# Chunked attention and two MLPs on one core: the order of the first pieces, and the engine of one conversion step

## The chip, the cores and the metric

The kernel runs on one core of a Trainium2 chip. The metric is the device time of one execution in microseconds (us); the median of several runs is given. The core's engines are TensorE (PE), VectorE (DVE), ScalarE (ACT), GpSimd (POOL) and SyncE (SP). Each runs its own instructions in the order in which the program issued them and waits at semaphores for the others; SP and POOL here mostly issue DMA transfers.

## What is computed

```python
# q, k, v: (4, 8, 576, 64); attention within chunks of 64 rows
scores = scale * q_c @ k_c.T ; attn = softmax(scores) ; out = attn @ v_c
x = out.transpose(0, 2, 1, 3).reshape(2304, 512)
# first MLP, d_ff = 1536
x = ((x @ w_a) * (x @ w_b)) @ w_out
# second MLP, d_ff = 2048, g a rational function of h
h = x @ w_in
g = (a0 + a1*h + a2*h*h + a3*h*h*h) / (1 + |b0|*|h| + |b1|*h*h + 1e-6)
return g @ w_out2
```

Weights come in 64 bits (f64 on the host) and are turned into f32 on the core.

## The kernel before

**Arithmetic.** A product of the MLPs is made of three passes: each operand is split into a high part (a rounded copy, ScalarE) and a low part (what is left, VectorE), and `mm3` (lines 250 to 252) adds high x high, high x low and low x high.

**Attention** goes in 18 units of 128 tokens (two chunks, eight heads). A unit's steps, with their letters in the table FIRST: k and q are transposed on TensorE and copied by ScalarE (line 328 and 330, letters k and q, copies kT and qT), scores are multiplied (345) and VectorE takes the row maximum and subtracts it (351, 353; S), ScalarE takes the exponential (359; X), VectorE sums and divides (364 to 367; E), the probabilities are transposed (375) and copied to pT (377; P), multiplied with v (392; V), with the high part of x copied by ScalarE (408), and the low part follows on VectorE (412; L). Units 0 to 2 are done ahead of the main loop; units 3 to 5 lie between its products.

**Weights.** A tile of weights is loaded as raw 64-bit words into one of four buffers (AHEAD = 4; SP queue, line 170) and converted in four pieces by `w_piece` (line 199; letter w): piece 0 makes two terms of the raw words, z on ScalarE (215) and c, the exponent term, on ScalarE (217) or VectorE (219); piece 1 takes the high part of the tile before (192, ScalarE) and shifts c (222, VectorE); piece 2 makes the last bits (224, ScalarE), takes the low part of the tile before (197, VectorE) and asks for another load; piece 3 adds the terms to an f32 tile (232, VectorE), which POOL stores to DRAM (234). A load into a raw buffer waits until the tile that lay there has been through pieces 0 and 2. Tiles are numbered in their order of use: tile 0 is the first of w_a, 1 the first of w_b, 2 the second of w_a, and so on; the number stands in the name of a converted tile (`w_a_2_361` is tile 2).

**Order.** The schedule is by hand: what the Python code issues first stands first in an engine's queue. Ahead of the main loop it is the table LOADS (first loads on SP) and then the table FIRST (lines 80 to 83). In FIRST a letter with a number is a step of a unit, `w` is the next piece of weights, `d4` is four idle products of the identity with itself on TensorE (`warm`, line 803), and `+k5` is a load. The main loop (885) makes, for each of the first pairs of tiles, the half products `ab` of w_a (a_s, the copy of it by ScalarE, line 888) and of w_b, 12 passes each; in the middle of each and after each stands `half()` (875), a stop at which the next pieces of weights and the due steps of attention are issued. How many pieces have been issued by stop n is in line 880.

**After 60 us** come the rest of attention, the second part of the first MLP and the second MLP, which the change does not touch.

Of the kernel before, what the change touches and what calls it, by code (L numbers as in the profile page):

```python
# [20 lines left out]
def chunk_attention_two_mlps(  # L21
# [56 lines left out]


    FIRST = (  # L80
        "k0 d2 q0 w w S0 w X0 k1 d2 w E0 q1 w S1 X1 P0 w k2 q2 E1 V0 w S2 X2 L0 P1 w +k5 +q5 w V1 d4 E2 w w +v3 +v4 +v5 "
        "L1 d2 P2 d4 w w V2 d4 L2 w w"
    ).split()
    LOADS = "k0 q0 w k1 q1 v0 w k2 q2 v1 w v2 w k3 q3 k4 q4".split()

    AHEAD = 4
    NWP = 12 - AHEAD
    AN = 1280

    SIZES = [256, 512, 512, 512, 512]  # L90
    START = [sum(SIZES[:j]) for j in range(len(SIZES))]
# [50 lines left out]
    order1 = [(n, i) for i in range(F1) for n in ("a", "b")]  # L142
    ordero = [("o", i) for i in range(F1)]
# [29 lines left out]
    def w_tile(key, dtype):  # L173
        at = w_at[key]
        if at < len(order1):
            pool, tag = p_w, f"w{at % NWP}"
        elif at < len(order1) + len(ordero):
            pool, tag = p_w, f"w{at - len(order1)}"
        else:
            pool, tag = p_w2, f"v{at - len(order1) - len(ordero)}"  # L180
        t = pool.tile([P, 2, DM], dtype, name=f"w_{key[0]}_{key[1]}_{at}", tag=tag)
        return t[:, 0], t[:, 1]

    def w_fetch_ahead(n):
        while n_cv[0] < n_cv[2] and n_cv[0] < n + (AHEAD if n_cv[0] < len(order1) else 2):
            w_fetch()

    def w_hi(n):
        if n in f32s:
            key = order[n]  # L190
            wt[key] = w_tile(key, F32R)
            nc.scalar.copy(wt[key][0], f32s[n].bitcast(F32))

    def w_lo(n):
        if n in f32s:
            hi, lo = wt[order[n]]
            nc.vector.tensor_tensor(lo, f32s.pop(n).bitcast(F32), hi.bitcast(F32), ALU.subtract)

    def w_piece():


        n, piece = divmod(n_cv[1], 4)
        n_cv[1] += 1
        key = order[n]
        if piece == 0:
            w_fetch_ahead(n)
            t = raws.pop(key)

            terms[n] = (t, *w_tile(key, I32))
        t, c, z = terms[n]  # L210
        hw = t[:, :, 1]
        lw = t.rearrange("p f t -> p (f t)").bitcast(U16).rearrange("p (f t) -> p f t", t=4)[:, :, 1]
        zz = z.bitcast(F16).rearrange("p (f t) -> p f t", t=2)
        if piece == 0:
            nc.scalar.activation(zz[:, :, 1], hw.bitcast(F32), AF.Copy, scale=2.0 ** -112)
            if 0 < n < len(order1) + len(ordero):
                nc.scalar.activation(c.bitcast(F32), hw.bitcast(F32), AF.Copy, scale=2.0 ** -112)
            else:
                nc.vector.tensor_scalar(c.bitcast(F32), hw.bitcast(F32), 2.0 ** -112, None, ALU.mult)
        elif piece == 1:  # L220
            w_hi(n - 1)
            nc.vector.tensor_scalar(c, c, 3, None, ALU.logical_shift_left)
        elif piece == 2:
            nc.scalar.activation(zz[:, :, 0].bitcast(U16), lw, AF.Copy, scale=2.0 ** -13)
            w_lo(n - 1)
            if n < len(order1):
                w_fetch_ahead(n + 1)
        else:
            w_fetch_ahead(n + 1)
            del terms[n]  # L230
            x = f32s[n] = p_io.tile([P, DM], I32, name="w_x", tag="io")
            nc.vector.tensor_tensor(x, c, z, ALU.add)
            if key in w1_d:
                nc.gpsimd.dma_start(out=w1_d[key], in_=x.bitcast(F32))

    def w_until(tiles):

        while n_cv[1] < min(4 * tiles, 4 * n_cv[2]):
            w_piece()

    def w_flush():

        n = n_cv[1] // 4 - 1
        if n in f32s:
            w_hi(n)
            w_lo(n)
# [20 lines left out]
    def tick(dt):  # L267

        now[0] += dt
        while todo:  # L270
            nxt = min(todo, key=lambda t: t[:2])
            if nxt[0] > now[0] + 1e-6:
                break
            todo.remove(nxt)
            nxt[2]()
# [363 lines left out]
    def a_tile(n):  # L639
        at = n_a[0] if n_a[0] + n <= AN else 0  # L640
        n_a[0] = at + n
        return a_ring[:, at:at + n]
# [232 lines left out]
    def half():  # L875


        n = n_half[0]
        n_half[0] += 1
        w_until(min(15 + 2 * n, 32) / 4 if n < 17 else (n + 18) / 4)  # L880
        if n_cv[1] == 32 or n_cv[1] == 4 * len(order1):
            w_flush()
        tick(0.5)
# [79 lines left out]
    for n, (j, i) in enumerate(places):  # L963
# [17 lines left out]
        if j == NB - 1:  # L981
# [4 lines left out]
            if i >= F1 - EARLY:  # L986
                if a_ring is None:
                    w_flush()
                    s_cv.close()
                    p_a = ctx.enter_context(tc.tile_pool(name="a", bufs=1, side="right", reuse_waits="tile"))  # L990
                    a_ring = p_a.tile([P, AN], F32, name="a_ring", tag="a_ring")
                step2(i - (F1 - EARLY))
# [32 lines left out]
```

## Time and profile before

| | us |
|---|---|
| median of 3 runs | 917.63 (916.88 to 918.42) |
| profiled execution | 916.23 |
| its span, first to last instruction | 914.5 |
| TensorE busy | 890.3 (97%) |
| VectorE busy | 722.2 (79%) |
| ScalarE busy | 612.9 (67%) |

The profile is one execution. The span is from the first to the last instruction, and the profiled execution's own time is 1.7 us longer. TensorE is busy nearly all the time; where it waits, and for whom, is read from the views by time, of which the rows are shown below.

### The profile page before, as it was taken

To read this page: it belongs to the slowest core of one execution; us is meant where nothing else is said; L and a number is where in the kernel's file an instruction comes from. 1 tells how busy PE (TensorE), PEld (TensorE's weight loads), DVE (VectorE), ACT (ScalarE), POOL (GpSimd) and SP (SyncE) were. 2 spreads that over 40 slices of the span, in tenths; PEclk is the share of its full clock that TensorE was granted. 3 is DMA by queue.
4 is the path that set the end of the run, shared out by engine and by line. 5 is a ranking of instruction groups with operands and counts; after the bars stand their busy time and mean duration, and the time that the engine had idled before them with its cause. 6 is when DMAs were issued, how large, how long until landed. Compare 5 with 4: busy or idle time off the path is not lost.

```text
span 914.5 us, 14768 instructions
## 1 busy us (share of the span) xinstructions
PE 890.3 (97%) x5532; PEld 787.9 (86%) x5532; DVE 722.2 (79%) x1321; ACT 612.9 (67%) x1105; POOL 63.8 (7%) x122
## 2 busy tenths in 40 slices
PE   5989999999999999999999999999999999999998
PEld 4888989989999999888886899888888888888997
DVE  6657788488888785677766599999889988988886
ACT  6757888355554552667766588877677767677775
POOL 0111111111111111000000000000000000000000
PEclk9999999999999999999999999999999999999999
DMA  9959996234343413777767110110020002000100
GB/s 244 272 174 256 255 237 169 95 127 153 122 144 121 149 57 111 257 246 252 256 228 252 60 46 1 40 42 1 1 92 1 1 1 80 1 1 1 47 1 35
DMA packets 107336, 105.82 MB, mean 116 GB/s; under 512 B 61441, under 2 KB 84481, under 8 KB 107265
## 3 DMA queue, kind: packets, MB, share of 16 engines
q1 hardware_dynamic: 99264, 79.71, 29.8%
q0 software_dynamic: 8000, 25.17, 7.7%
q8 instruction: 43, 0.70, 0.3%
q14 instruction: 29, 0.23, 0.1%
HBM read 74.98 MB, written 29.88 MB: 115 GB/s over the span
## 4 chain that ended last, share of the span: by engine, by line
PE 90%; DVE 3%; DMA 3%; ACT 2%; issue 1%; SPq 0%; DVEq 0%; ACTq 0%
PE acc L251 7%; PE h L252 7%; PE h L250 7%; PE h L251 7%; PE acc L250 7%; PE acc L252 7%; PE acc L668 5%; PE acc L669 5%; PE acc L674 5%; PE ab L250 4%; PE ab L251 3%; PE ab L252 3%; PE y L251 2%; PE y L250 2%; PE y L252 2%; PE q L250 2%
## 5 line engine op out<-in xcount | busy, mean ns | idle before, releaser
L252 PE MATMUL h<-y,w_i 128*128 128x512 f32 (+1 forms) x320 | 118.0, 369 | 0.0
L250 PE MATMUL h<-y,w_i 128*128 128x512 f32 (+1 forms) x320 | 117.9, 368 | 0.0
L251 PE MATMUL h<-y,w_i 128*128 128x512 f32 (+1 forms) x320 | 117.8, 368 | 0.0
L732 ACT ACTIVATE a_ring<-h 128x512 f32<-128x512 f32 (+1 forms) x80 | 44.1, 552 | 88.6 <-PE h L252 88.6
L668 PE MATMUL acc<-g_hi,w_o 128*128 128x512 f32 (+1 forms) x240 | 88.9, 377 | 2.8 <-ACT g_hi L654 2.1
L576 ACT COPY s<-y 128x384 f32<-128x384 f32 x72 | 34.5, 479 | 80.2 <-PE y L252 79.0
L669 PE MATMUL acc<-g_hi,w_o 128*128 128x512 f32 (+1 forms) x240 | 87.4, 371 | 0.0
L735 DVE SCALAR_TENSOR_TENSOR u<-u,cb_t,a_ring 128x512 f32<-128x512 f32 (+1 forms) x80 | 55.7, 696 | 30.8 <-ACT u L733 29.9
L251 PE MATMUL acc<-w_o,g_hi 128*128 128x512 f32 x191 | 75.3, 394 | 0.0
L250 PE MATMUL acc<-w_o,g_hi 128*128 128x512 f32 x191 | 74.9, 392 | 0.0
L252 PE MATMUL acc<-w_o,g_lo 128*128 128x512 f32 x191 | 74.3, 389 | 0.0
L250 PEld LDWEIGHTS h<-y,w_i 128*128 128x128 f32 x320 | 60.1, 188 | 8.9
L251 PEld LDWEIGHTS h<-y,w_i 128*128 128x128 f32 x320 | 60.1, 188 | 8.7
L252 PEld LDWEIGHTS h<-y,w_i 128*128 128x128 f32 x320 | 60.1, 188 | 7.4
L656 DVE TENSOR_TENSOR g_lo<-g_raw,g_hi 128x512 fp32r<-128x512 f32 (+1 forms) x60 | 38.0, 636 | 31.8 <-ACT g_hi L654 17.7
L674 PE MATMUL acc<-g_lo,w_o 128*128 128x512 f32 (+1 forms) x237 | 59.9, 374 | 0.7 <-DVE g_lo L656 0.6
L734 ACT ACTIVATE t<-h,ca_t 128x512 f32<-128x512 f32 (+1 forms) x80 | 59.0, 738 | 0.0
L745 DVE SCALAR_TENSOR_TENSOR u<-u,r 128x512 f32<-128x512 f32 (+1 forms) x80 | 50.5, 632 | 9.5 <-ACT r L744 9.5
L737 DVE SCALAR_TENSOR_TENSOR t<-t,ca_t,h 128x512 f32<-128x512 f32 (+1 forms) x80 | 55.5, 694 | 2.8
L668 PEld LDWEIGHTS acc<-g_hi,w_o 128*128 128x128 f32 x240 | 45.1, 188 | 13.9 <-ACT g_hi L654 4.5
L744 ACT ACTIVATE r<-r,nlsh 128x512 f32<-128x512 f32 (+1 forms) x80 | 54.6, 682 | 2.6
L743 ACT ACTIVATE r<-u,nlsh 128x512 f32<-128x512 f32 (+1 forms) x80 | 55.5, 694 | 0.3
(195 smaller groups left out, 2415.5 us busy)
## 6 DMA issues: line engine op xcount, KB each, us to landing
w_raw<-in_moe_w_out_dram SPq DMA_DIRECT2D x28, 512.0 KB, 3.7
g_d<-g POOLq DMA_DIRECT2D x72, 192.0 KB, 2.5
g_raw<-g_d SPq DMA_DIRECT2D x48, 256.0 KB, 4.0
w_raw<-in_moe_w_in_dram SPq DMA_DIRECT2D x16, 512.0 KB, 3.9
w_raw<-in_moe_w_a_dram SPq DMA_DIRECT2D x12, 512.0 KB, 5.1
w_raw<-in_moe_w_b_dram SPq DMA_DIRECT2D x12, 512.0 KB, 5.1
out_dram<-o SPq DMA_DIRECT2D x18, 256.0 KB, 2.4
y_d<-ys POOLq DMA_DIRECT2D x16, 256.0 KB, 3.7
```

The lines of the kernel that those rows point to most:

```text
L250: nc.tensor.matmul(ps, wh, xh, start=first, stop=False, **kw)
L251: nc.tensor.matmul(ps, wh, xl, start=False, stop=False, **kw)
L252: nc.tensor.matmul(ps, wl, xh, start=False, stop=last, **kw)
L668: nc.tensor.matmul(acc[j][d], wh, gh, start=i == 0, stop=False)
L669: nc.tensor.matmul(acc[j][d], wl, gh, start=False, stop=False)
L674: nc.tensor.matmul(acc[j][d], cols(w, d)[0], gl, start=False, stop=last)
L734: nc.scalar.activation(t, ps, AF.Identity, scale=ca_t[:, 3:4], bias=ca_t[:, 2:3])
L735: nc.vector.scalar_tensor_tensor(u, u, cb_t[:, 0:1], ah, ALU.add, ALU.mult)
L737: nc.vector.scalar_tensor_tensor(t, t, ca_t[:, 1:2], ps, ALU.add, ALU.mult)
L743: nc.scalar.activation(r, u, AF.Ln, scale=2.0 ** -LSH, bias=nlsh[:, 0:1])
L744: nc.scalar.activation(r, r, AF.Exp, scale=-1.0, bias=nlsh[:, 1:2])
L745: nc.vector.scalar_tensor_tensor(u, u, 1.0 + 1e-6, r, ALU.add, ALU.mult)
```

## The change

Three things are altered.

1. The table FIRST, from P1 on: the two pieces of weights that stood ahead of V1 and its idle products now stand behind the normalisation of unit 2 (E2), so E2 comes two pieces earlier, and P2 and V2 come earlier against the pieces too; the loads of v for units 3 to 5 now come ahead of the pieces that ask for tiles 6 and 7. The idle products behind V1, P2 and V2 become 2, 1 and 2; they were 4 and 2, 4, and 4. The count of pieces, 15, is the same.
2. Line 880: by each stop of the main loop up to the 32nd piece, two more pieces have been issued.
3. The exponent term c of tiles 2 to 5 is made by VectorE instead of ScalarE (`C_ACT` lists the tiles that stay on ScalarE).

```diff
     FIRST = (
-        "k0 d2 q0 w w S0 w X0 k1 d2 w E0 q1 w S1 X1 P0 w k2 q2 E1 V0 w S2 X2 L0 P1 w +k5 +q5 w V1 d4 E2 w w +v3 +v4 +v5 "
-        "L1 d2 P2 d4 w w V2 d4 L2 w w"
+        "k0 d2 q0 w w S0 w X0 k1 d2 w E0 q1 w S1 X1 P0 w k2 q2 E1 V0 w S2 X2 L0 P1 +k5 +q5 V1 d2 E2 w w "
+        "+v3 +v4 +v5 P2 d1 L1 w V2 d2 w L2 w w w w"
     ).split()
...
+    C_ACT = (1, *range(6, 36))
...
-            if 0 < n < len(order1) + len(ordero):
+            if n in C_ACT:
                 nc.scalar.activation(c.bitcast(F32), hw.bitcast(F32), AF.Copy, scale=2.0 ** -112)
             else:
                 nc.vector.tensor_scalar(c.bitcast(F32), hw.bitcast(F32), 2.0 ** -112, None, ALU.mult)
...
-        w_until(min(15 + 2 * n, 32) / 4 if n < 17 else (n + 18) / 4)
+        w_until(min(17 + 2 * n, 32) / 4 if n < 17 else (n + 18) / 4)
```

In the changed kernel every line from 90 on is two higher: L170 is L172, L215 is L217, L330 is L332, L888 is L890.

The queue of SP, from the loads of k and q of unit 5 on. The two `w_raw` rows are the raw loads of tiles 6 and 7, the v rows those of units 3, 4 (in two halves) and 5. Before:

```order
L319 DMA kqv<-in_k_dram 128x8x64
L319 DMA kqv<-in_q_dram 128x8x64
L170 DMA w_raw<-in_moe_w_a_dram 128x4x256
L319 DMA kqv<-in_v_dram 128x8x64
L319 DMA kqv<-in_v_dram 64x8x64 x2
L319 DMA kqv<-in_v_dram 128x8x64
L170 DMA w_raw<-in_moe_w_b_dram 128x4x256
```

After:

```order
L321 DMA kqv<-in_k_dram 128x8x64
L321 DMA kqv<-in_q_dram 128x8x64
L321 DMA kqv<-in_v_dram 128x8x64
L321 DMA kqv<-in_v_dram 64x8x64 x2
L321 DMA kqv<-in_v_dram 128x8x64
L172 DMA w_raw<-in_moe_w_a_dram 128x4x256
L172 DMA w_raw<-in_moe_w_b_dram 128x4x256
```

The load of tile 6 moved behind the three units' v, 768 KB.

ScalarE around the end of the first half product (a_s is its copy). The line of `w_raw` with w_a_4 is the first piece of tile 4. Before:

```order
L408 CAST x_hi<-at 128x4x64 x2
L192 CAST w_a_2_455<-w_x 128x512
L224 ACTIVATE w_b_3_425<-w_raw 128x512
L888 COPY a_s<-ab 128x384
L215 ACTIVATE w_a_4_490<-w_raw 128x512
L217 ACTIVATE w_a_4_490<-w_raw 128x512
L330 COPY kT<-at 128x512
```

After:

```order
L410 CAST x_hi<-at 128x4x64 x2
L226 ACTIVATE w_a_2_389<-w_raw 128x512
L217 ACTIVATE w_b_3_442<-w_raw 128x512
L194 CAST w_a_2_445<-w_x 128x512
L226 ACTIVATE w_b_3_442<-w_raw 128x512
L217 ACTIVATE w_a_4_472<-w_raw 128x512
L890 COPY a_s<-ab 128x384
L194 CAST w_b_3_483<-w_x 128x512
L226 ACTIVATE w_a_4_472<-w_raw 128x512
L332 COPY kT<-at 128x512
```

Tile 4's first piece moved ahead of a_s, and tile 3's high part and tile 4's last bits ahead of the copy kT of unit 3; the second line of tile 4's first piece is on VectorE.

ScalarE one half product later, around unit 5's copies and the a_s that follows. Before:

```order
L192 CAST w_a_4_564<-w_x 128x512
L224 ACTIVATE w_b_5_540<-w_raw 128x512
L330 COPY qT<-at 128x512
L888 COPY a_s<-ab 128x384
L215 ACTIVATE w_a_6_613<-w_raw 128x512
L217 ACTIVATE w_a_6_613<-w_raw 128x512
L359 ACTIVATE e<-e 128x512
L192 CAST w_b_5_648<-w_x 128x512
```

After:

```order
L194 CAST w_a_4_533<-w_x 128x512
L226 ACTIVATE w_b_5_507<-w_raw 128x512
L332 COPY qT<-at 128x512
L332 COPY kT<-at 128x512
L217 ACTIVATE w_a_6_564<-w_raw 128x512
L219 ACTIVATE w_a_6_564<-w_raw 128x512
L332 COPY qT<-at 128x512
L890 COPY a_s<-ab 128x384
L194 CAST w_b_5_606<-w_x 128x512
L226 ACTIVATE w_a_6_564<-w_raw 128x512
L361 ACTIVATE e<-e 128x512
```

Tile 6's first piece (both its lines stay on ScalarE) moved ahead of unit 5's qT, of a_s and of tile 5's high part.

## Rows read from the trace of the kernel before

**Rows 1.** The page, part 4: the chain that ended last, by engine.

```profile
PE 90%; DVE 3%; DMA 3%; ACT 2%; issue 1%; SPq 0%; DVEq 0%; ACTq 0%
```

**Rows 2.** Busy time by stage: window, us, each engine, clock granted, DMA share, GB/s.

```profile
26.67:60.00 33.33, 29.10 (x330) 25.29 (x329) 21.91 (x51) 22.00 (x43) 4.42 (x8) 0.95 1.01 269
60.00:160.00 100.00, 99.20 (x1188) 90.63 (x1191) 77.86 (x163) 79.15 (x151) 16.71 (x31) 1.00 0.79 215
300.00:914.00 614.00, 607.06 (x2880) 520.77 (x2878) 498.68 (x858) 424.08 (x744) 20.50 (x38) 1.00 0.25 83
```

**Rows 3.** TensorE in order of time: start, us, line, count, [idle before, releaser].

```profile
19.90 0.79 PE L392 MATMUL at<-pT,kqv 64*64 64x64 f32 x32 [2.07 <-ACT pT L377]
20.62 2.32 PE L807 MATMUL at<-ident 128*128 128x128 f32 x12
22.74 1.06 PE L375 MATMUL at<-ident,t 128*128 128x128 f32 x4
...
26.67 0.42 PE L250 MATMUL ab<-x_hi,w_a 128*128 128x384 f32 x1
...
31.49 0.66 PE L328 MATMUL at<-ident,kqv 128*128 128x128 f32 x4 [0.32 <-ACT kT L330]
...
47.51 0.66 PE L375 MATMUL at<-ident,e 128*128 128x128 f32 x4 [2.29 <-DVE e L367]
```

**Rows 4.** ScalarE in order of time, at the first a_s, and tile 6.

```profile
29.29 0.48 ACT L888 COPY a_s<-ab 128x384 f32<-128x384 f32 x1 [1.57 <-PE ab L252]
29.66 0.79 ACT L215 ACTIVATE w_a<-w_raw 128x512 f16<-128x512 f32 x1
30.31 0.65 ACT L217 ACTIVATE w_a<-w_raw 128x512 f32<-128x512 f32 x1
30.85 0.58 ACT L330 COPY kT<-at 128x512 f32<-128x512 f32 x1
31.32 0.64 ACT L192 CAST w_b<-w_x 128x512 fp32r<-128x512 f32 x1
31.84 0.82 ACT L224 ACTIVATE w_a<-w_raw 128x512 uint16<-128x512 uint16 x1
32.50 0.58 ACT L330 COPY qT<-at 128x512 f32<-128x512 f32 x1
...
38.04 0.79 ACT L215 ACTIVATE w_a<-w_raw 128x512 f16<-128x512 f32 x1
```

**Rows 5.** SP's queue in order of time: loads of tile 4, tile 6, unit 5's v.

```profile
23.58 1.63 SPq L170 DMA_DIRECT2D w_raw<-in_moe_w_a_dram  x1
...
27.65 2.69 SPq L170 DMA_DIRECT2D w_raw<-in_moe_w_a_dram  x1
...
33.72 1.07 SPq L319 DMA_DIRECT2D kqv<-in_v_dram  x1
```

**Rows 6.** The same three loads: KB, and us from issue to landing.

```profile
w_raw<-in_moe_w_a_dram SPq DMA_DIRECT2D x1, 512.0 KB, 5.5
...
w_raw<-in_moe_w_a_dram SPq DMA_DIRECT2D x1, 512.0 KB, 7.4
...
kqv<-in_v_dram SPq DMA_DIRECT2D x1, 256.0 KB, 5.4
```

**Rows 7.** VectorE in order of time, unit 4's maximum to its division.

```profile
39.17 0.76 DVE L351 TENSOR_REDUCE m<-at 128x4 f32<-128x256 f32 x2 [0.27 <-PE at L345]
...
40.50 0.42 DVE L222 TENSOR_SCALAR w_a<-w_a 128x512 int32<-128x512 int32 x1
40.83 0.69 DVE L197 TENSOR_TENSOR w_b<-w_x,w_b 128x512 fp32r<-128x512 f32 x1
...
46.76 0.69 DVE L367 TENSOR_TENSOR e<-e,s 128x512 f32<-128x512 f32 x1
```

**Rows 8.** Busy time by stretch, columns as in rows 2, after the 2.29 us wait.

```profile
48.60:51.90 3.30, 3.30 (x42) 2.75 (x41) 2.51 (x6) 1.11 (x3) 0.54 (x1) 0.50 0.99 348
```

## The prediction, made before the changed kernel was timed

> **What bounds the kernel now.** I read the chain of waits first: 90% of the path that ends last is TensorE, the remaining tenth is spread over VectorE, DMA and ScalarE [rows 1]. The table by stage says where that tenth is. From 60 us on TensorE is busy 99.2 of 100 us and 607 of 614 us, so whatever delay or lead it has at 60 us is carried to the end one for one; between 26.67 and 60 us it is busy only 29.1 of 33.3 us while the DMA share is 1.01, so the transfer engines have nothing left there [rows 2]. The change works before 60 us only, so this stretch decides. In TensorE's own order of time [rows 3] the reader is to see four places: unit 1's last attention product (V1, 19.90), which waited 2.07 us for ScalarE; the twelve passes of idle products behind it; the first product of the main loop at 26.67; and two waits after it, 0.32 us at 31.49 (the transposes of unit 4's k, for the copy kT of unit 3) and 2.29 us at 47.51 (unit 4's probabilities, for VectorE).
>
> **First term: the start.** Six, four and four idle products become two, one and two. The six took 2.12 us, 0.35 each (20.62 to 22.74) [rows 3]; unit 2's transposes behind them can start up to four products, 1.4 us, earlier, since the normalisation E2 that they need stands on VectorE one conversion earlier now. Behind the transposes the copy to pT, V2's products and its x_hi copies are a chain of ScalarE and TensorE that no idle product shortens. Bounds for the first main product: nothing gained, or all nine idle products, 9 x 0.35 = 3.2 us. I take 1.5 us, the part ahead of the transposes, so it starts near 25.2. The second idle group that is cut costs nothing while TensorE waits for pT anyway.
>
> **Second term: tile 4 meets its load.** The main loop now asks for two more pieces of weights at its first stop, so the first conversion of tile 4 (L215) stands ahead of the copy a_s (L888) on ScalarE. Steps on ScalarE, from start to start [rows 4]: L888 0.37, L215 0.65, L217 0.54, L330 0.47, L192 0.52, L224 0.66. V2's x_hi copies would end near 25.0; then come L224, L215, L192 and L224 (2.5 us), so tile 4 is asked for near 27.5. Its load is issued at 23.58 [rows 5] and lands 5.5 us later [rows 6], at 29.1; nothing ahead of it in SP's queue moves. ScalarE therefore waits 1.6 us, and behind it are a_s, the high part of tile 3, L224 and only then kT of unit 3: 29.1 + 0.65 + 0.37 + 0.52 + 0.66 = 31.3, done 0.58 us later, 31.9. TensorE's k transposes of unit 4 need the bank that this copy frees; they stood at 31.49 [rows 3]. The lead of 1.5 us has become a lag of 0.4 us, and L217, now on VectorE for this tile, has spared nothing.
>
> **Third term: tile 6 meets a load that moved back.** In SP's queue the loads of v for units 3 to 5 now stand ahead of tile 6 (the order rows on SP show it). Before, tile 6 was issued at 27.65 and landed 7.4 us later, 35.05; the last v was issued at 33.72 and landed 5.4 us later, 39.1 [rows 5, 6]. The same bytes go through engines that are full, so tile 6 now lands last of them, at 39.1 instead of 35.05. ScalarE asked for it at 38.04, after a_s of unit 1 [rows 4]; now it asks one stop sooner: 31.3 (kT) + 0.47 + 0.65 (L215 of tile 5) + 0.47 + 0.47 + 0.52 + 0.66 + 0.47 + 0.47 = 35.5. It stands still for 3.6 us, and behind it are unit 5's qT, a_s and the high part of tile 5: 39.1 + 0.65 + 0.54 + 0.47 + 0.37 = 41.1, done 0.64 later, 41.8. VectorE's low part of tile 5 (L197, 0.60 from start to start) waits for that, and behind it in VectorE's queue stands the maximum of unit 4's scores (L351): near 42.5, where it stood at 39.17 [rows 7]. That is 3.3 us late.
> From there to the end of unit 4's normalisation VectorE had no idle time: 39.17 to 46.76 + 0.69 = 47.45 [rows 7]. After the change the same kinds stand between (one L222, one L197, one L232, two units' sums), so the step stays 8.3 us and unit 4's transposes on TensorE go from 47.51 to 50.8. **+3.3 us.**
>
> **Fourth term: behind that.** VectorE does two conversions (L232, L197) ahead of unit 5's normalisation, which may come another 0.8 us later against TensorE; before, TensorE was slow there itself, since the granted clock fell to 0.50, 1.2 of its 2.4 GHz, between 48.6 and 51.9 [rows 8], after the 2.29 us wait. Bounds: -0.9 us if that slow stretch does not come back, +0.8 us if all of VectorE's extra shows. I take +0.2 us.
>
> **Edits that cost nothing.** The four exponent terms on VectorE (tiles 2 to 5) are 0.43 us each at most, by the row of L222, the same kind and size [rows 7]; they lie where VectorE waits for ScalarE's tile or the raw load. If that cover were gone it would be 4 x 0.43 = 1.7 us. ScalarE's saving of 4 x 0.54 = 2.2 us ends in the two waits for loads. POOL's queue keeps its order but for two neighbours, and the stores of converted tiles, two pieces earlier, share the engines with tile 6: 256 KB at 269 GB/s [rows 2] is 1 us more on its landing at most, and none less.
>
> Sum: +3.3 + 0.2 = +3.5 us. The profiled execution took 916.23 us (span 914.5 us), 1.4 us below the median of the runs, 917.63; the stretch is the same in both, so I add it to the median: **921.1 us**.
>
> **Rivals.** *Tile 6 is there in time (not slower).* If the engines fetch tile 6 beside the v's, it lands before 35.5 and ScalarE does not stop: 35.5 + 0.65 + 0.54 + 0.47 = 37.2, a_s waits for its product until about 38.1, the high part of tile 5 ends at 39.1, the maximum starts at 39.7 instead of 39.17: +0.5 us from the second term, with the fourth +0.7: 918.3 us, no difference that can be measured. It decides at a landing of 36 us; each us after that is a us of the end. Against it: the three loads in rows 5 landed in the order of their issue, at 29.1, 35.05 and 39.1 [rows 5, 6]. The Trainium skill ("DMA: Bandwidth & Descriptors", section "Two DMAs through the same engine are not ordered") says that transfers on one engine are not finished in order as a rule. By it the landing need not be last; the trace does not bear it out for these loads. Chance 0.15.
> *The early start survives (faster).* If tile 4 landed before 27.5 and tile 6 before 35.5, the 1.5 us of the first term would reach 47.51, the 2.29 us wait there would be met by a VectorE that is ahead by as much, and the slow stretch might go as well: -1.5 - 0.9, 915.2 us. For it speaks only that one store of 256 KB leaves the engines later; against it rows 6 and the DMA share of 1.01. Chance 0.09.
> *The slow clock comes more often (slower still).* TensorE would now stand still twice for 2.5 us or more, before unit 5's scores and before 50.8. A wait of 2.29 us was followed by 3.3 us at 1.2 GHz [rows 8]; a second such stretch behind 50.8, where TensorE is again what is late, costs half of it, 1.65 us, and with the 0.8 of the fourth term 2.5: 923.6 us. The Trainium skill ("TensorE: Matmul & The Clock Gate", section "Why this matters for your kernels") warns of idle time between bursts for that reason. A slow stretch that lies ahead of the 50.8 wait is hidden by it, as is one at the start, by tile 4. Chance 0.14.
> The forecast itself has 0.62.
>
> **How the numbers follow.** The forecast reaches from a landing of tile 6 at 37.5 (+1.9) to one at 40.1 (+4.5). With the first rival's 918.3 at the low end and most of the third's at the high end the range is 918.3 to 924.0 us; about 2 in 10 is left out, the faster case first. A measurement of this kernel tells about 0.2%, 1.8 us, from no change. Faster by more: the second rival, 0.09. Within: the first rival and a little of the forecast's low end, 0.19. Slower: the rest, 0.72.
>
> **What the profile after will show.** The first main product near 25.2, not 26.67. ScalarE idle 1.6 us before L215 of tile 4 with a DMA named, and about 3.6 us before tile 6's near 39.1, again with a DMA named: this is the step on which the forecast stands. Tile 6 issued after the last v. The maximum of unit 4 near 42.5 on VectorE, unit 4's transposes near 50.8 on TensorE, and from 60 us on everything the same but 3.5 us later. If ScalarE has no wait for tile 6, or the first product is not earlier, that step is wrong; if TensorE at 60 us is not later, the whole forecast is.

## The result, and the profile after

| | before | after |
|---|---|---|
| median, us | 917.76 (916.83 to 918.82, 6 runs) | 923.81 (921.50 to 926.12, 6 runs) |
| ratio to before, 95% interval | | 1.0072 [1.0056, 1.0087] |
| profiled execution, us | 916.23 | 921.83 |
| its span, us | 914.5 | 920.0 |

The change makes the kernel 6.05 us slower. The forecast was 921.1 us with a range of 918.3 to 924.0: the direction was right, the size too small. The ratio on 917.63, the median that the forecast was made against, gives 924.2, just above the range; a second comparison (after_again, below) has the kernel at 926.04. The profiled executions stand 5.50 us apart in span.

Page of the kernel after, its head, parts 1, 3 and 4 (the chain answers to [rows 1]):

```profile
span 920.0 us, 14732 instructions
...
PE 890.8 (97%) x5514; PEld 787.8 (86%) x5514; DVE 724.4 (79%) x1325; ACT 611.5 (66%) x1101; POOL 64.0 (7%) x122
...
q8 instruction: 43, 0.70, 0.3%
...
PE 87%; DVE 5%; DMA 4%; ACT 2%; issue 1%; SPq 0%; DVEq 0%; ACTq 0%
```

TensorE is busy as long as before (890.8 us), with 18 records less (nine products of two passes each); its share of the chain fell from 90% to 87%, and VectorE and DMA gained 2% and 1%. Nothing new is computed: 5.5 us more of waiting. Busy time by stage, columns as in [rows 2]; the last row is a stretch that the forecast had no row for:

```profile
26.00:60.00 34.00, 25.21 (x271) 22.42 (x271) 22.13 (x50) 19.36 (x38) 4.96 (x9) 0.86 0.89 254
60.00:160.00 100.00, 99.23 (x1187) 90.95 (x1186) 75.35 (x159) 77.11 (x149) 15.85 (x30) 1.00 0.78 213
305.60:919.60 614.00, 605.90 (x2875) 518.77 (x2873) 498.45 (x857) 424.27 (x743) 20.59 (x38) 1.00 0.25 83
359.70:379.70 20.00, 16.94 (x131) 16.09 (x130) 10.98 (x24) 7.22 (x15) 1.63 (x3) 1.00 0.53 168
```

and the same piece of work in the kernel before, which stood 4.7 us earlier:

```profile
355.00:375.00 20.00, 18.08 (x139) 17.24 (x138) 11.04 (x25) 7.74 (x17) 1.62 (x3) 1.00 0.55 185
```

Two places lose time. Ahead of 60 us TensorE is busy 25.21 of 34.00 us (before: 29.10 of 33.33, [rows 2]). And some 300 us later it is busy 16.94 us of twenty where it was busy 18.08: another 1.1 us.

**The early part.** TensorE, ScalarE, SP's queue and VectorE of the kernel after, in order of time (start, us, line, count, [idle before, releaser]); they answer to [rows 3], [rows 4], [rows 5] and [rows 7]:

```profile
20.45 0.79 PE L394 MATMUL at<-pT,kqv 64*64 64x64 f32 x32 [2.07 <-ACT pT L379]
...
25.65 0.67 PE L252 MATMUL ab<-x_hi,w_a 128*128 128x384 f32 x1
...
32.54 0.66 PE L330 MATMUL at<-ident,kqv 128*128 128x128 f32 x4 [1.11 <-ACT kT L332]
...
45.00 1.45 PE L347 MATMUL at<-kT,qT 64*64 64x64 f32 x32 [4.63 <-DVE e L355]
...
52.10 0.66 PE L377 MATMUL at<-ident,e 128*128 128x128 f32 x4 [0.54 <-DVE e L369]
```

```profile
29.75 0.80 ACT L217 ACTIVATE w_a<-w_raw 128x512 f16<-128x512 f32 x1 [1.47 <-DMA w_raw<-in_moe_w_a_dram]
...
31.93 0.55 ACT L332 COPY kT<-at 128x512 f32<-128x512 f32 x1
...
35.63 0.59 ACT L332 COPY kT<-at 128x512 f32<-128x512 f32 x1
40.49 0.78 ACT L217 ACTIVATE w_a<-w_raw 128x512 f16<-128x512 f32 x1 [4.27 <-DMA w_raw<-in_moe_w_a_dram]
```

```profile
23.35 0.54 SPq L172 DMA_DIRECT2D w_raw<-in_moe_w_a_dram  x1
...
27.96 6.36 SPq L321 DMA_DIRECT2D kqv<-in_v_dram  x4
34.43 1.04 SPq L172 DMA_DIRECT2D w_raw<-in_moe_w_a_dram  x1
```

```profile
43.78 0.75 DVE L353 TENSOR_REDUCE m<-at 128x4 f32<-128x256 f32 x2
...
46.87 0.69 DVE L369 TENSOR_TENSOR e<-e,s 128x512 f32<-128x512 f32 x1
```

Read them from the bottom of the cause: the three v's, in four loads, leave SP at 27.96, tile 6 only at 34.43 (27.65 before). ScalarE has finished kT at 35.63 + 0.59 and then stands still for 4.27 us until tile 6 is there, at 40.49, with a DMA named. VectorE reaches the maximum of unit 4 at 43.78 instead of 39.17, and TensorE unit 4's transposes at 52.10 instead of 47.51: +4.59. Between these two steps lie 8.32 us, before 8.34, so nothing on that piece of the way costs more than it did.

**The second place.** ScalarE at the end of the first MLP, before and after. Four rows each: the last copy s, the first piece of w_in that waits for its load, the first halves of the gate that are read back from memory (g_raw), and the first copy ys of the product with w_out:

```profile
357.21 0.48 ACT L576 COPY s<-y 128x384 f32<-128x384 f32 x1 [2.39 <-PE y L252]
...
367.03 0.80 ACT L215 ACTIVATE w_i<-w_raw 128x512 f16<-128x512 f32 x1 [1.55 <-DMA w_raw<-in_moe_w_in_dram]
368.79 0.77 ACT L654 CAST g_hi<-g_raw 128x256 fp32r<-128x256 f32 x2 [0.96 <-DMA g_raw<-g_d]
...
377.90 0.37 ACT L681 COPY ys<-acc 128x256 f32<-128x256 f32 x1 [0.36 <-PE acc L674]
```

```profile
361.90 0.48 ACT L578 COPY s<-y 128x384 f32<-128x384 f32 x1 [2.39 <-PE y L254]
...
372.18 0.78 ACT L217 ACTIVATE w_i<-w_raw 128x512 f16<-128x512 f32 x1 [2.00 <-DMA w_raw<-in_moe_w_in_dram]
374.63 0.77 ACT L656 CAST g_hi<-g_raw 128x256 fp32r<-128x256 f32 x2 [1.68 <-DMA g_raw<-g_d]
...
383.72 0.37 ACT L683 COPY ys<-acc 128x256 f32<-128x256 f32 x1 [0.35 <-PE acc L676]
```

From the first row to the last it is 20.69 us before and 21.82 after. I call this the gate stretch, since here the gate, the product of x @ w_a and x @ w_b, is written to memory (L490, POOL) and read back (L647, SP). The waits that end with a DMA grew: 1.55 to 2.00 us for w_in, 0.96 to 1.68 us for the gate. The instructions are the same in both kernels and in the same order; why should they wait longer? The trace lists all transfers, the chip's own among them, and one of these stands in another place. Transfers issued or running in four short stretches: the last store of the gate, and the packet of the queue that the profile calls "instruction" (queue, packets, MB, share; issue, KB, us to landing):

```profile
g_d<-g POOLq DMA_DIRECT2D x1, 192.0 KB, 2.8
...
q8 instruction: 1, 0.02, 21.9%
```

```profile
g_d<-g POOLq DMA_DIRECT2D x1, 192.0 KB, 4.1
...
q8 instruction: 1, 0.02, 20.2%
```

Before, the packet ran at 360.9 us, beside the store before the last (issued at 359.63, landed 4.3 us later), and the last store, issued at 361.94, landed in 2.8 us. After, it ran at 367.8, behind the issue of the last store at 366.65, which landed in 4.1 us; the store before it took 2.4. SP's load of w_out and its four reads of the gate follow in the two kernels at

```profile
363.74 0.50 SPq L170 DMA_DIRECT2D w_raw<-in_moe_w_out_dram  x1
364.36 1.79 SPq L647 DMA_DIRECT2D g_raw<-g_d  x4
```

```profile
368.45 1.41 SPq L172 DMA_DIRECT2D w_raw<-in_moe_w_out_dram  x1
369.98 1.78 SPq L649 DMA_DIRECT2D g_raw<-g_d  x4
```

The reads are 5.62 us apart, where everything ahead of them, the issue of w_out included, is 4.7 apart. The late store is not what holds them: the first read leaves at 369.98, and the store lands only at 366.65 + 4.12 = 370.77. What stands ahead of the read in SP's queue is the issue of the load of w_out, and that took 1.41 us instead of 0.50: +0.91 of the +0.93 by which the read is late. The packet ran from 367.84 for 1.62 us, to 369.46; the issue ended 0.40 us behind it, at 369.86. In all six profiles of the table below that have nine idle products this issue took 1.14 to 1.69 us and ended 0.38 to 0.41 us behind the packet; in the other eight it took 0.50 or 0.51. The first read then lands 4.56 us after its issue (4.33 before), so it is 1.15 us late, and the gate stretch is 1.13 longer. Why SP's issue ends only behind the packet, no run shows.

What is this packet? 43 of them carry 0.70 MB, 16 KB each, and TensorE has 2 x 5532 records (products and weight loads), 257 for each packet. I took it for the load of TensorE's next instructions. The change leaves out nine idle products, each of two records of products and two of weight loads, so that 36 records less stand ahead of every later piece of the program: each load of instructions comes 36 records later in it. Against the last copy s, the packet starts 3.62 to 3.79 us later in the six profiles of the table that have the idle products of before, and 5.73 to 6.10 us later in the six with nine. The Trainium skill, page "Runtime: NRT & Kernel Launch", section "Instruction fetch mechanics", says that an engine's instructions are refilled by its own DMA queue in blocks of 16 KiB, 256 instructions, and that the cost of a block is mostly hidden. The size and the count agree with the trace. "Hidden" does not hold for SP's issue behind the packet, if the experiments below bear this reading out.

### The profile page after: what moved, and what is told of

Same layout as the page of the kernel before. It is cut to its first block, busy times and chain, and to the rows that moved or that the text cites. A ratio compares the mean times of both kernels' runs of the same rounds, so it can differ in the third digit from the quotient of the medians.

```text
span 920.0 us, 14732 instructions
## 1 busy us (share of the span) xinstructions
PE 890.8 (97%) x5514; PEld 787.8 (86%) x5514; DVE 724.4 (79%) x1325; ACT 611.5 (66%) x1101; POOL 64.0 (7%) x122
## 4 chain that ended last, share of the span: by engine, by line
PE 87%; DVE 5%; DMA 4%; ACT 2%; issue 1%; SPq 0%; DVEq 0%; ACTq 0%
PE acc L253 7%; PE h L254 7%; PE h L252 7%; PE acc L252 7%; PE h L253 7%; PE acc L254 7%; PE acc L670 5%; PE acc L671 5%; PE acc L676 4%; PE ab L252 3%; PE ab L254 3%; PE ab L253 3%; PE y L254 2%; PE y L253 2%; PE y L252 2%; PE q L252 2%
```

## The experiments

The theory in two parts: (1) **late load**, tile 6's load stands behind the v's on SP, as forecast; (2) **code load**, nine idle products fewer move an instruction load onto the last store of the gate. (The texts put on record name this store as what is delayed; the rows above put the cost one step further, at SP's issue of w_out and the reads of the gate behind it.) The rivals: (3) **slow clock**, fewer idle products let TensorE's clock fall more often; (4) the exponent term on VectorE, which was costed at nothing, costs something. The first four kernels were chosen before the second place was found, so what is on record for them knows (1) and (3) only.

All profiles were read at the same rows of ScalarE: the x_hi copy of unit 4 (54.95 us before), the last copy s (357.21) and the first ys (377.90). "Early" is the first one's start against the kernel before's, "gate" the time from the second to the third. "Idle" is the number of idle products in the table FIRST. Medians stand against the kernel before in the same comparison.

| kernel | idle | v against tile 6 | median, us | against before | early, us | gate, us |
|---|---|---|---|---|---|---|
| before | 18 | behind | 917.63 | | 0 | 20.69 |
| after | 9 | ahead | 923.81 | +6.05 | +4.74 | 21.82 |
| after_again | 9 | ahead | 926.04 | +8.78 | +6.40 | 23.74 |
| ask15 | 9 | ahead | 922.29 | +5.03 | +5.75 | 22.71 |
| a_idle | 18 | ahead | 922.92 | +6.18 | +6.73 | 20.65 |
| v_late | 9 | behind | 921.67 | +4.41 | +1.55 | 22.27 |
| v_late_idle | 18 | behind | 918.15 | +1.71 | +1.15 | 20.66 |
| b_vfirst | 18 | ahead | 918.76 | +1.50 | +4.07 | 20.62 |
| b_idle | 9 | behind | 919.03 | +2.29 | +0.38 | 22.15 |
| b_cact | 18 | behind | 915.32 | -1.12 | -1.30 | 20.72 |
| b_cact_vend | 18 | behind, last | 916.07 | -0.39 | +0.31 | 20.69 |
| vend_k4 | 9 | behind, last | 916.93 | +0.19 | -1.62 | 21.55 |
| vend_k4_pad | 18, 9 of them moved | behind, last | 915.79 | -0.95 | -1.19 | 21.46 |
| vend_k4_pad18 | 27 | behind, last | 915.62 | -0.82 | 0.00 | 20.57 |

"Early" and "gate" are of one execution each and the median is of many, so they need not add up. The profiled execution of the kernel before is a quick one: 1.4 us under its median, and a copy that the change does not touch, ScalarE's first x_hi at 16.37, stood 0.16 to 1.40 us later in the thirteen other profiles (1.02 in v_late, 0.56 in the kernel after). The profiled executions of v_late, v_late_idle and vend_k4 lie 2.3, 1.7 and 2.4 us under their medians, those of ask15 and vend_k4_pad18 1.6 and 1.7 above, so "early" flatters the first three.

### The kernel after once more: after_again

No edit.

> The changed kernel once more, for a second profile and its spread. Late-load theory: the time of an execution goes with the landing of tile 6, so the profile shows ScalarE's wait before tile 6 ending earlier or later than 40.49 by about as much as this profile's span differs from 920.0, and the runs spread over 3 us or more, where the other three kernels spread over 2. Slow-clock theory: the wait ends where it did, and the span goes with the length of the slow stretches.

Measured: 926.04 us (922.12 to 926.60, 6 runs), ratio 1.0084 [1.0069, 1.0099]. Its profiled execution took 925.81 us. ScalarE's wait for tile 6, and one stretch of the table by stretch (columns as in [rows 2]):

```profile
42.15 0.79 ACT L217 ACTIVATE w_a<-w_raw 128x512 f16<-128x512 f32 x1 [3.62 <-DMA w_raw<-in_moe_w_a_dram]
```

```profile
378.10:381.50 3.40, 3.40 (x18) 3.40 (x17) 1.79 (x4) 1.65 (x4) 0.00 (x0) 0.50 0.63 201
```

The wait is a little shorter than in the first profile (3.62 against 4.27 us) but ends later, at 42.15 instead of 40.49: the loads ran late from the start (16.37 became 17.77). And the gate stretch takes 3.05 us more than before, not 1.13. In it TensorE waited 0.77 and 1.68 us for the gate's halves, the last wait up to 377.08, and from 378.1 to 381.5 the granted clock is 0.50, 1.2 of the 2.4 GHz, with TensorE busy all the time. So here the late reads were followed by a stretch at the lower clock; half of its 3.4 us, 1.7 us, is an estimate of what it costs. That is most of what this profile has beyond the first. The text on record expected the time to go with the end of the wait for tile 6; that end moved by 1.66 us and the span by 4.0, so the rest comes from elsewhere. It also expected a spread of 2 us for the other three kernels of this comparison; v_late, b_vfirst and ask15 spread over 4.1 to 5.4.

### v behind tile 6 again: v_late

```diff
-        "+v3 +v4 +v5 P2 d1 L1 w V2 d2 w L2 w w w w"
+        "P2 d1 L1 w V2 d2 w +v3 +v4 +v5 L2 w w w w"
```

> The changed kernel with one thing undone: the loads of v for units 3 to 5 stand behind tile 6's load again. Late-load theory: tile 6 lands some 4 us sooner, near 36 to 37, about when ScalarE asks for it, so the wait of 4.27 us goes; what is left is tile 4's wait of 1.5 us, and the kernel ends about 1 us above the kernel before, near 918.6 us, with the small spread of before. Slow-clock theory (the fewer idle products and the waits they leave lower TensorE's clock, and that costs the 5 us): still 3 us or more above before, with slow stretches of the clock as long as in the changed kernel. Conversion theory (four more steps on VectorE cost it): still 3 us or more above.

Measured: 921.67 us (919.37 to 923.51, 6 runs), ratio 1.0044 [1.0028, 1.0059]: +4.41 against before where the kernel after has +6.05 and +8.78, but 3 us more than expected. Most of the early delay is gone (+1.55 instead of +4.74 and +6.40), so the late load is a cause; half of the miss, 1.58 us, is in the gate stretch, 22.27 us. This run sent me there. The profiled execution (919.37) is the quickest of the six, so what the median has beyond it is in no profile. What remains early is the next load behind the v's, tile 7's, for which ScalarE now waits 2.19 us:

```profile
43.29 0.79 ACT L217 ACTIVATE w_b<-w_raw 128x512 f16<-128x512 f32 x1 [2.19 <-DMA w_raw<-in_moe_w_b_dram]
```

### v ahead of tile 6 in the kernel before: b_vfirst

```diff
-  w V1 d4 E2 w w +v3 +v4 +v5 "
+  w V1 d4 E2 w +v3 +v4 +v5 w "
```

> The kernel before with one thing done: the loads of v for units 3 to 5 go ahead of tile 6's load; idle products, stops and conversion engines as before. Late-load theory: tile 6 lands near 39 to 40.5 where it is asked for near 38, so ScalarE waits 1 to 2.5 us and the end is 1 to 2 us later, near 919.3 us: less than in the change, since the asking is one stop later. Slow-clock and conversion theories: no difference from before.

Measured: 918.76 us (917.21 to 921.26, 11 runs), ratio 1.0021 [1.0011, 1.0031], inside what the late-load theory expected. The move of the v's alone costs, though in the median 1.5 us only: before, ScalarE came to tile 6 later and had less to wait for. The profiled execution (919.83 us) is above its median, with +4.07 early and the gate stretch of the kernel before, 20.62.

### The weight pieces due as before: ask15

```diff
-        w_until(min(17 + 2 * n, 32) / 4 if n < 17 else (n + 18) / 4)
+        w_until(min(15 + 2 * n, 32) / 4 if n < 17 else (n + 18) / 4)
```

> The changed kernel with the stops of before (15 + 2n pieces instead of 17 + 2n): tile 6 is asked for one stop later, behind the copy a_s and unit 5's qT, and its load lands as late as in the change. Late-load theory: ScalarE still waits some 2.5 us for tile 6, but less stands behind it, and the kernel ends 1 to 2 us above before, near 919.3 us. Slow-clock theory: as the change, 5 to 6 us above before, since the idle products are the same.

Measured: 922.29 us (918.49 to 923.90, 6 runs), ratio 1.0042 [1.0026, 1.0058]. The late-load theory expected far less, and its profile shows why it missed. TensorE's transposes of units 4 and 5, and the stretch behind the first:

```profile
48.25 1.12 PE L377 MATMUL at<-ident,e 128*128 128x128 f32 x4 [3.15 <-DVE e L369]
...
52.42 1.11 PE L377 MATMUL at<-ident,e 128*128 128x128 f32 x4 [1.13 <-DVE e L369]
```

```profile
47.40:57.60 10.20, 8.22 (x57) 7.16 (x58) 8.71 (x20) 5.01 (x12) 1.62 (x3) 0.50 0.94 297
```

With fewer pieces due, tile 6's load is still late (asked behind the v's, ScalarE waits 3.00 us), but less of VectorE's work stands behind it: unit 4's transposes are only 0.74 us late (48.25 against 47.51). Then the clock is at 0.50 for 10.2 us, where before it was for 3.3 [rows 8], and at the x_hi copy the delay is 5.75. Half of the 6.9 us more is at most 3.5, and a further wait for VectorE is 1.13; before, unit 5's transposes had none. So in this execution rival (3) did up to 3.5 of the 5.0 us lost behind these transposes. The median, +5.03, is what the slow-clock theory had expected for this kernel; 2.0 us of it are in the gate stretch, and the profiled execution (923.90) is the slowest of the six. One execution can't tell how often the slow stretch comes; the kernel after's own rows (8.32 against 8.34 us, above) do not have it.

### Only the idle products: b_idle and a_idle

The kernel before with the idle products of the kernel after, and the reverse:

```diff
 # b_idle, against before
-  w V1 d4 E2 w w +v3 +v4 +v5 "  "L1 d2 P2 d4 w w V2 d4 L2 w w"
+  w V1 d2 E2 w w +v3 +v4 +v5 "  "L1 P2 d1 w w V2 d2 L2 w w"
 # a_idle, against after
-  V1 d2 E2 w w "  "+v3 +v4 +v5 P2 d1 L1 w V2 d2 w
+  V1 d6 E2 w w "  "+v3 +v4 +v5 P2 d4 L1 w V2 d4 w
```

> The kernel before with the idle products of the kernel after: nine fewer (18 fewer records on TensorE), nothing else moved. Code-load theory (the change also moves TensorE's 16 KB instruction loads 36 records later in the program, so that one of them meets the last store of the gate at about 367 us instead of the one before it): nothing lost by 60 us, and +1.0 to +2.8 us lost between 345 and 375 us, so about 918.4 to 920.2 where the kernel before takes 917.4. Late-load theory alone (tile 6's load behind unit 3 to 5's v): no change, within 0.5 us, since no load moves. Slow-clock theory: a loss of 1 us or more ahead of 60 us.

> The kernel after with the idle products of the kernel before: nine more, at the places where it leaves them out. Code-load theory: the shift against before at 60 us stays at +4 to +6 us, and nothing more is lost between 345 and 375 us (the store that meets the instruction load is the one before the last again), so 1.0 to 2.8 us less than the kernel after. Late-load theory alone: the same as the kernel after. Slow-clock theory: close to the kernel before.

Measured: b_idle 919.03 us (917.34 to 921.32, 11 runs), ratio 1.0025 [1.0014, 1.0035]; a_idle 922.92 us (919.86 to 924.36, 6 runs), ratio 1.0068 [1.0049, 1.0087]. The pair of rows at the two ends of the gate stretch, and last store and instruction load, of b_idle:

```profile
357.43 0.48 ACT L576 COPY s<-y 128x384 f32<-128x384 f32 x1 [2.39 <-PE y L252]
...
379.58 0.37 ACT L681 COPY ys<-acc 128x256 f32<-128x256 f32 x1 [0.36 <-PE acc L674]
```

```profile
g_d<-g POOLq DMA_DIRECT2D x1, 192.0 KB, 4.1
...
q8 instruction: 1, 0.02, 17.0%
```

and of a_idle:

```profile
363.60 0.48 ACT L578 COPY s<-y 128x384 f32<-128x384 f32 x1 [2.39 <-PE y L254]
...
384.25 0.37 ACT L683 COPY ys<-acc 128x256 f32<-128x256 f32 x1 [0.36 <-PE acc L676]
```

```profile
g_d<-g POOLq DMA_DIRECT2D x1, 192.0 KB, 2.7
...
q8 instruction: 1, 0.02, 20.4%
```

b_idle is 0.23 us behind the kernel before at 357 us and 1.68 at the first ys: nine idle products that nobody waits for, left out ahead of 30 us, cost 1.45 us at 370 us, and 2.29 in the median. The instruction load moved from 360.9 to 363.5, behind the issue of the last store, which landed in 4.1 us instead of 2.8. a_idle puts the products back: the load (367.3) is ahead of the last store (368.35), the store lands in 2.7 us, the gate stretch is 20.65, and the early delay stays, +6.73. In the median the 1.0 to 2.8 us expected do not show: +6.18 stands against +6.05 and +8.78 for the kernel after, in other comparisons; here the profile alone decides. The two causes are separate, and rival (3) as the explanation of the whole falls: with the idle products back, TensorE is no earlier at 60 us. That the packet carries TensorE's instructions is thereby as good as shown, since in b_idle nothing but TensorE's number of instructions differs. In b_idle too the store is a neighbour and not the link: SP's issue of w_out took 1.32 us instead of 0.50, and the first read of the gate left at 365.42, ahead of the store's landing at 366.27.

### Both suspects away: v_late_idle

The two edits of v_late and a_idle together.

> The kernel after with both suspects taken away: tile 6's load asked ahead of unit 3 to 5's v, and the nine idle products of before put back. If the late load and the instruction load are two separate costs that add, nothing is lost between 345 and 375 us and some +1 to +2 us are left at 60 us, so +1 to +2 us against the kernel before, 1.5 to 2.5 us less than with the v's moved alone (+4.4). If the instruction load is not a cost of its own, the same +4.4 us.

Measured: 918.15 us (916.45 to 921.36, 12 runs), ratio 1.0020 [1.0008, 1.0032]: +1.7 us, as expected if the two add. Gate stretch 20.66, early +1.15, with the wait for tile 7's load still there.

### Only the exponent term: b_cact

```diff
-            if 0 < n < len(order1) + len(ordero):
+            if n == 1 or 5 < n < len(order1) + len(ordero):
```

> The kernel before with one part of the change alone: the exponent term of tiles 2 to 5 on VectorE. No load is asked in another order and no idle product is left out. Both theories: nothing lost; from 0 to -0.7 us, since ScalarE is spared 4 x 0.54 us in the stretch before 60 us. If the part that was costed at nothing is a cost, +0.5 to +1.7 us.

Measured: 915.32 us (913.73 to 916.62, 11 runs), ratio 0.9989 [0.9978, 1.0000]. Rival (4) falls, as far as the kernel before can tell; this part of the change is a gain of about 1 us, if it is anything. ScalarE is spared the work and waits instead, 2.04 us, for the load behind the v's:

```profile
43.65 0.80 ACT L215 ACTIVATE w_b<-w_raw 128x512 f16<-128x512 f32 x1 [2.04 <-DMA w_raw<-in_moe_w_b_dram]
```

### v asked last: vend_k4 and its paddings, b_cact_vend

In all four the loads of v for units 3 to 5 come behind those of tiles 6 and 7, at the end of FIRST. vend_k4 is the kernel after, with pieces due from 15 + 2n and unit 4's k and q behind tiles 4 and 5. The padded ones add idle products in waits of TensorE ahead of 25 us. b_cact_vend is b_cact with the v's last.

```diff
 # vend_k4, against after
-  L0 P1 +k5 +q5 V1 d2 E2 w w " "+v3 +v4 +v5 P2 d1 L1 w V2 d2 w L2 w w w w"
+  L0 P1 +k4 +q4 +k5 +q5 V1 d2 E2 w w " "P2 d1 L1 w V2 d2 w L2 w w w w +v3 +v4 +v5"
-  ... v2 w k3 q3 k4 q4".split()
+  ... v2 w k3 q3".split()
 # vend_k4_pad, against vend_k4
-  "k0 d2 ...  +k5 +q5 V1 d2
+  "d5 k0 d2 ...  +k5 +q5 d4 V1 d2
 # vend_k4_pad18, against vend_k4
-  "k0 d2 ... w w S0 ... q1 w S1 ... V0 w S2 ... +k5 +q5 V1 d2
+  "d7 k0 d2 ... w w d1 S0 ... q1 w d1 S1 ... V0 w d2 S2 ... +k5 +q5 d6 V1 d3
```

> The kernel after with unit 3 to 5's v loads asked at the end of the first pieces (behind the loads of tiles 6 and 7 and those ahead), unit 4's k and q behind the loads of tiles 4 and 5, and weight pieces due from 15 + 2n as before. Late-load theory: ScalarE no longer waits some 4 us for tile 6, so the early part ends 1 to 2 us sooner than in the kernel before. Code-load theory: it has nine idle products fewer than the kernel before, so 1.0 to 2.8 us are lost between 345 and 375 us all the same; in all -1.0 to +1.8 us against before.

> The same kernel with nine idle products more, put where TensorE waits anyway (five ahead of the first transposes, four ahead of unit 1's V), so that its instruction loads fall where they do in the kernel before. Code-load theory: nothing is lost between 345 and 375 us, so 1.0 to 2.8 us faster than the kernel without them, and about 2 us faster than the kernel before (near 915.4). Theory without code loads: the same time as the kernel without them.

> The kernel with v asked last and k and q of unit 4 behind tiles 4 and 5, with eighteen idle products more than without padding (nine more than the padded one before it), all in waits of TensorE ahead of 25 us. Code-load theory: the 16 KB instruction load now comes some 2 us earlier, ahead of the last store of the gate altogether, so nothing is lost between 354 and 372 us, where the kernel with nine more lost 0.75 us: 914.8 to 915.4 us where before takes 916.7. Theory without code loads: the same as with nine.

> The kernel before with two edits: the exponent term of tiles 2 to 5 on VectorE, and unit 3 to 5's v asked behind the loads of tiles 6 and 7 at the end of the first pieces. With the exponent term alone ScalarE waited 2.04 us for tile 7's load, which stands behind the three v's. If a load behind the v's is what the end of the early part hangs on, that wait goes and the kernel is 1 to 2 us faster than before; if the exponent term alone did it, the same -1.1 us; if v asked last is late for its own products, slower than that.

Measured: vend_k4 916.93 us, ratio 1.0008 [0.9996, 1.0020]; vend_k4_pad 915.79, 0.9992 [0.9983, 1.0001]; vend_k4_pad18 915.62, 0.9993 [0.9984, 1.0002]; b_cact_vend 916.07, 0.9990 [0.9977, 1.0002]. With the v's last ScalarE waits for no load between 24 and 53 us in vend_k4, and unit 4's transposes come earlier than in the kernel before:

```profile
46.83 0.66 PE L377 MATMUL at<-ident,e 128*128 128x128 f32 x4 [2.42 <-DVE e L369]
```

That is the other half of the evidence for the late load: its whole delay goes, +4.74 becomes -1.62, though vend_k4 also has k and q of unit 4 moved and the pieces due as in ask15 (which alone left +5.75). As for the code load, vend_k4 and its first padding keep what the theory says in the median (1.1 us apart), but not in the profile: the padded kernel's gate stretch is 21.46, 0.77 more than before's. Its instruction load ran at 360.6, at the very time at which its last store was issued (360.6), and ended ahead of SP's issue of w_out, which took 0.50 us; the reads of the gate then took 5.1 us to land instead of 4.3. With eighteen more it ran at 356.2, ahead of both stores, and the stretch is 20.57, as expected; but the same kernel then lost 1.2 us further on, between the first ys and 500 us, and its next instruction load, at 375.9, stands just ahead of a read of the gate that took 5.1 us to land, 3.9 before. It is the same pattern: the issue of that read took 1.48 us instead of 0.38 and ended 0.37 us behind the packet. Its median, 915.62, is just above the 914.8 to 915.4 expected. Padding moves the loads; it does not remove them. b_cact_vend, -0.39 us, shows neither the 1 to 2 us of a freed wait nor, clear of the noise, a loss against b_cact.

None of these kernels is faster than the kernel before by more than the measurement of 0.2% can tell. b_cact, the best median against its own comparison, is one line and touches no order.

## Why the forecast was right in direction and too small

**First term (the start), held.** It said that the first main product would start near 25.2; it started at 25.65, 1.0 us earlier than the 26.67 of [rows 3], though V1 had started 0.55 later. The forecast had 1.5 us for it. As forecast, the gain was spent at the next load.

**Second term (tile 4), held.** ScalarE waited 1.47 us for tile 4's load, forecast 1.6, and the k transposes of unit 4 came at 32.54 with a wait for kT named: 1.05 us late where +0.4 was forecast. The difference is the landing of tile 4: ScalarE could start at 29.75 instead of 29.1, since the load took 6.4 us from its issue at 23.35, not the 5.5 of before. Why it took longer is open; the loads that landed between 19 and 26 us were earlier than before, not later.

**Third term (tile 6), right in mechanism, too small.** Each link is there: tile 6 issued behind the last v, ScalarE idle with a DMA named, the maximum of unit 4 late, 8.3 us to the transposes. The sum was +3.3 and it came to +4.59, and in the other profiles of the same order to more (ScalarE freed at 42.15 in after_again and 42.49 in a_idle). Of the 4.59, 0.56 was in place at the first x_hi copy, ahead of any change. The step that failed is the sentence "The same bytes go through engines that are full, so tile 6 now lands last of them, at 39.1". Tile 6 did land last, but at 40.47, 1.4 us later, and they are not the same bytes. All transfers from the issue of tile 4's load to the landing of the last of these loads, before and after:

```profile
DMA packets 8461, 4.31 MB, mean 278 GB/s; under 512 B 6558, under 2 KB 8219, under 8 KB 8461
```

```profile
DMA packets 8824, 4.80 MB, mean 281 GB/s; under 512 B 6675, under 2 KB 8516, under 8 KB 8822
```

The rate is the same, 278 and 281 GB/s, but 4.80 MB went through instead of 4.31, and 0.49 MB at 280 GB/s is 1.75 us; part of it is made up by the start at 23.35 instead of 23.58. One more store of a converted tile (256 KB) is among it, since the pieces come earlier: POOL's stores went from 0.99 to 1.25 MB, SP's loads from 3.32 to 3.53. The store is 0.95 us at that rate; for the 0.21 MB of loads I have no cause, and a window that ends later takes in more in any case. No run takes the store away, so this share is argued and not shown. I had this store as "1 us more on its landing at most" and took zero of it for the forecast. With engines that have nothing left, a transfer that is moved earlier should have been counted with the bytes ahead of the awaited load.
The landing order that the first rival rested on is settled too: the v's landed at 35.8 to 39.0 and tile 6 after them, at 40.5, so here the loads finished in the order of issue. The Trainium skill ("DMA: Bandwidth & Descriptors", section "Two DMAs through the same engine are not ordered") warns that this is not guaranteed; none of these rows shows it broken.

**Fourth term (behind that), held as a sum.** +0.2 was forecast; the shift went from +4.59 at unit 4's transposes to +4.74 at the x_hi copy. Both of its parts came, and that they cancelled is luck: no slow stretch of the clock came back behind 52.10, and in its place TensorE waited 1.40 us for VectorE at unit 5's transposes, where it had not waited before:

```profile
55.95 0.63 PE L377 MATMUL at<-ident,e 128*128 128x128 f32 x4 [1.40 <-DVE e L369]
```

**"From 60 us on everything the same but 3.5 us later", false.** This is the second step that failed, one whose size I could not have known, but should have left room for: leaving out instructions was costed as the time of these instructions. It also moved the loads of all later instructions, one of them onto SP's loads at the gate, and the gate stretch, put at nothing, grew by 1.1 us in the profile of the kernel after, 1.5 in b_idle and 3.0 in after_again, where a slow stretch of the clock followed. Summed over the profile: 4.74 early (of it 0.56 in place at 16.9 us, before any change acts) + 1.12 in the gate stretch - 0.36 elsewhere = 5.50.

**The rivals.** Tile 6 in time: no, the wait was 4.27 us. The early start survives: no. The slow clock more often: not in the profile of the kernel after on the path that counts, though the lower clock is there for longer, 6.8 us twice; the second time it lies ahead of the 52.10 wait and is hidden by it:

```profile
42.46:49.28 6.82, 4.28 (x41) 4.14 (x42) 6.01 (x16) 5.06 (x10) 0.54 (x1) 0.50 0.97 217
```

It did show as a cost in ask15 (early) and in after_again (at 378 us); its price, half of a stretch, is the same estimate there as in the forecast, and its place was another.

**"Edits that cost nothing".** The exponent terms on VectorE: right, b_cact is no slower. The stores of converted tiles: the 1 us at most was the better guess, and zero was taken; see the third term.

**Adding the stretch to the median.** I added +3.5 from one execution to the median of before. The profile of before was a quick one, 1.4 us under that median, and the profile of the kernel after is 2.0 us under its own, so a difference of two profiles, 5.5 us, is not the difference of the medians, 6.05. In three profiles with the v's ahead of tile 6 and the pieces due as in the kernel after, tile 6's wait ended at 40.49, 42.15 and 42.49. That a load on the path makes the kernel's time vary more is not shown: the kernel after ran from 921.5 to 926.6 over two comparisons, and the kernel before from 914.5 to 919.6 over all of them.

## What to carry to other kernels

Where a profile shows the transfer engines with nothing left, count bytes, not places in a queue: what will land ahead of the awaited load, stores included, divided by the rate of that stretch. Ask of a load that is moved back not only whether it has slack now, but whether its reader is moved forward in the same edit. And an edit that only adds or drops instructions still moves the instruction loads of everything behind it: look at where these stand against the few transfers, and the issues of transfers, that are on the path, before and after, and if a change costs time in a place that it does not touch, look there first.

## What the runs showed of the chip that I had not expected

TensorE's instructions come in 43 packets of 16 KB, 0.9 to 1.8 us each in the gate stretches read here, on the transfer engines that carry the kernel's own data. A store that went beside one landed 1.3 to 1.9 us later (4.1 against 2.8 us for the last store of the gate, 4.3 against 2.4 for the one before it). An issue on SP that met one took 1.1 to 1.7 us instead of 0.5, and ended some 0.4 us behind it. In six profiles with the idle products of before the gate stretch took 20.62 to 20.72 us; in six with nine fewer 21.55 to 23.74. The two padded kernels show that it is the place of the packet that counts and not the number of products: 21.46 with the packet beside the last store, 20.57 with it ahead of both. Nine idle products of 0.35 us, put where nobody waits, decided over 0.9 to 3.0 us, some 340 us later.
